# Routing a batch in small pieces: its ranks in an ordinary PSUM bank, its gate and tables spread over the pairs behind it

## The chip, the cores and the metric

The kernel runs on one core of a Trainium2 chip. The metric is the time of one execution on the device in microseconds (us), the median of several runs. The engines have their own instruction queues and run side by side: TensorE (PE; its weight loads are shown as PEld), VectorE (DVE), ScalarE (ACT), GpSimd (POOL) and SyncE (SP), which issues most of the DMA transfers here. Matrix products land in PSUM, in banks of 512 fp32 numbers a partition; everything else lies in SBUF.

## The reference

Three layers, one behind the other, all in fp32:

```
# 1. attention with a memory, B=4 batches, H=8 heads, S=576, D=64
scores = q @ k.T / 8, causal;  a = softmax(scores);  local = a @ v
q_p = where(q > 0, q, exp(q) - 1) + 1
mem = (q_p @ M_prev) / (q_p @ z_prev + 1e-6)
x = g * mem + (1 - g) * local            # g = sigmoid(beta), a head each
# 2. mixture of experts on x as (2304, 512): the best of 8 experts
logits = x @ w_gate;  e = argmax(logits);  gate = softmax(logits)[e]
eom = sigmoid(x @ w_output_gate)
x = gate * eom[e] * (relu(x @ w1[e]) @ w2[e])
# 3. a dense layer
h = relu(x @ w_in);  out = (h * h) @ w_out
```

## The kernel before

**Attention in pairs of heads.** The work of the first layer is cut into 16 pairs: 4 batches, each with 4 pairs of heads. A pair passes four lanes, each a part of the generator `pair`: `prep` (load `kraw` and `qraw`, split them into a high and a low part, `ex` and `rq` on ScalarE), `front` (scores into the banks `sc`, their maxima `negm` on VectorE, the exponentials `a` on ScalarE), `back` (transposes `ptl`, `pt`; the memory product `pm` and its `xm`; the product with v into `pva` and `pvb`, copied to `pvs`; the transposes `ppt` of `pvs`; `tl` on VectorE (line 359), and `xb` = `tl` + `xm` on GpSimd (line 361)), and `end` (store `xb` to `x_dram`, transposes `pxt` to `xTg`, and the gate's product `plg` into `lgT`). In each period of about 12.5 us four successive pairs are worked on at once, one in each lane; the table `PLAN` of 19 steps says in which order the lanes take their steps. A scheduler then sets the final static order on each engine by a model of its own.

**Banks.** Two adjoining banks of PSUM form one wide place (`c.wide`, one buffer): a pair's last-row scores `psl` use it, and the ranks `prank` of a batch use it too. The other six banks are ordinary ones in rotation (`c.bank`).

**Routing of a batch.** When the last pair of a batch has gone through `end`, the next pair's `end` turns the batch's gate products (`plt`), and runs `route_batch` to its end: the one-hot choice `oh`, matrix products that count the ranks of tokens among those of the same expert (`prank`), the gate's softmax (`dd`, `zs`, `eo`, `so`) and its split into three bf16 numbers `sp`, and from the ranks `rk`, `rs` the tables `rblk`, `roff`, `ohoff`. The `yield`s in `route_batch` mean nothing here, since `drain` runs it through at once. The scheduler nevertheless mixes its instructions with those of the pairs.

**Early routing.** After the third batch, `route_early` (begun in the first pair of the fourth batch, finished in its second) chooses the blocks of tokens that the experts start on. It works on the tables of the first three batches: `eeq`, then the five parts of `eval` (two from token numbers `tokv`, three from the split gate `sp`; line 604), then on TensorE two runs of `eperm` with `ohoff` (line 609: the first of the token numbers, the second of the gate), of which `etp`, `egidx` and `esel` are read out, and an indirect DMA on GpSimd's queue gathers the rows `xg` by `egidx`. The transposes `ptx` of `xg` begin the experts, while the last pairs end. The fourth batch's routing and the rest follow among the experts, and then the dense layer.

Of the kernel before, what the change touches and what calls it, by code (L numbers as in the profile page):

```python
# [9 lines left out]
F32 = mybir.dt.float32  # L10
F32R = mybir.dt.float32r
BF16 = mybir.dt.bfloat16
I32 = mybir.dt.int32
# [121 lines left out]
def attention(tc, c, q, k, v, x_dram, pools):  # L135
# [31 lines left out]
    def pair(b, hp, lgT):  # L167
# [56 lines left out]
        def scores(js):  # L224
            banks = [bank(f"sc{js[0]}{h}") for h in range(2)]
            off = [sum((i + 1) * P for i in js[:t]) for t in range(len(js))]
            o, n = off[-1] + js[-1] * P, len(js)
            mask = c.maskd.unsqueeze(1).to_broadcast((P, n, P))
            for h in range(2):
                r = slice(64 * h, 64 * h + 64)  # L230

                def product(qx, kx, start, stop):
                    for i, j in enumerate(js):
                        nk = (j + 1) * P
                        lhs, rhs = (qx[:, h], kx[:, h]) if len(qx.shape) == 3 else (qx[r], kx[r])
                        nc.tensor.matmul(banks[h][:, off[i]:off[i] + nk], lhsT=lhs[:, j * P:nk], rhs=rhs[:, 0:nk],
                                         start=start and i == 0, stop=stop and i == n - 1)

                if stacked:
                    product(q2, k2, True, False)  # L240
                else:
                    product(qh, kh, True, False)
                    product(qh, kl, False, False)
                for i_, j in enumerate(js):
                    nk = (j + 1) * P
                    last = nc.tensor.matmul(banks[h][:, off[i_]:off[i_] + nk], lhsT=qlz[i][:, h, j * P:nk], rhs=kh[:, 0:nk], start=False, stop=False)
                if not stacked:
                    nc.tensor.matmul(banks[h][:, o - (n - 1) * P:o + P], lhsT=c.identb, rhs=mask, start=False, stop=True)
            with tc.issue_after(last.ins):
                for h in range(2) if stacked else ():  # L250
                    nc.tensor.matmul(banks[h][:, o - (n - 1) * P:o + P], lhsT=c.identb, rhs=mask, start=False, stop=True)  # L251
            views = [(banks[h][:, off[i]:off[i] + (j + 1) * P], h, j) for i, j in enumerate(js) for h in range(2)]
            for psv, h, j in views:
                nc.vector.tensor_reduce(out=negm[:, h, j:j + 1], in_=psv, axis=AX.X, op=ALU.max, negate=True)  # L254
            for psv, h, j in views:
                nk = (j + 1) * P
                nc.scalar.activation(a[:, h, aoff[j]:aoff[j] + nk], psv, AF.Exp, bias=negm[:, h, j:j + 1],  # L257
                                     accum_out=ssum[:, h, j:j + 1])
# [93 lines left out]
        for j0, j1 in ((0, 4), (4, 5)):  # L352
            n = j1 - j0
            pt = bank(f"ppt{j0}")
            for j in range(j0, j1):
                transpose(nc, pt[:, (j - j0) * P:(j - j0 + 1) * P], pvs[i][:, j * P:(j + 1) * P], c.ident)
            ptv = pt[:, 0:n * P].rearrange("p (j h e) -> p j h e", j=n, h=2)
            tl = ow.tile([P, 4, 2, D], F32, tag="tl", name="tl")
            nc.vector.tensor_mul(tl[:, 0:n], ptv, clv[:, j0:j1].unsqueeze(3).to_broadcast((P, n, 2, D)))
            xv = xb[:, j0:j1].rearrange("p j (h e) -> p j h e", h=2)  # L360
            (nc.vector if EV["xb"] == "v" or end else nc.gpsimd).tensor_add(xv, tl[:, 0:n], xm[:, j0:j1])
        yield "back"

        if pend:
            b0, l0 = pend.pop()
            logits(b0, l0)
            drain(c.route(b0))
        cs = slice(hp * P, (hp + 1) * P)
        nc.sync.dma_start(out=x_dram[b * S:b * S + 512, cs].rearrange("(j p) f -> p j f", p=P), in_=xb[:, 0:4])
        nc.sync.dma_start(out=x_dram[b * S + 512:(b + 1) * S, cs], in_=xb[0:LAST, 4])  # L370
# [16 lines left out]
        if end:  # L387
            logits(b, lgT)
        elif hp == H // 2 - 1:
            pend.append((b, lgT))  # L390
        elif b == B - 1:
            if hp == RE0:
                next(c.route_early, None)
            elif hp == RE0 + 1:
                for t in c.route_early:
                    if t is None:
                        yield

    pend = []

    def logits(b, lgT):
        pl = bank("plt")
# [12 lines left out]
    def drain(g):  # L415
        for _ in g:
            pass
# [13 lines left out]
    ends = ("end", "back", "front", "prep")  # L431
    for t in range(-2, n):
        lanes = [steps(gens[t + i - 1], ends[i]) if 0 <= t + i - 1 < n else None for i in range(4)]
        for lane in c.plan:
            if lanes[lane] is not None:
                next(lanes[lane], None)
        for lane in lanes[::-1]:
            if lane is not None:
                drain(lane)
# [54 lines left out]
def route_batch(tc, c, b, wk):  # L494
    nc = tc.nc
    cs = slice(b * NB, (b + 1) * NB)
    sh = (P, NB, E)
    lg, lo = c.lg[:, cs, 0:E], c.lg[:, cs, E:2 * E]
    oh = c.oh[:, cs]

    def t3(name):
        return wk.tile([P, NB, E], F32, tag=name, name=name, bufs=1)

    def t2(name, dt=F32):
        return wk.tile([P, NB], dt, tag=name, name=name, bufs=1)

    mx, m2, zs, so = t2("mx"), t2("m2"), t2("zs"), t2("so")
    dd, eo = t3("dd"), t3("eo")
    tt = c.tt[b % 2]
    tx = tt[:, :, 0:E]  # L510
    nc.scalar.activation(eo, lo, AF.Exp, scale=-1.0)
    nc.vector.tensor_reduce(out=mx, in_=lg, axis=AX.X, op=ALU.max)
    mxb = mx.unsqueeze(2).to_broadcast(sh)
    yield "f"
    nc.vector.tensor_tensor(out=tx, in0=lg, in1=mxb, op=ALU.is_equal)
    nc.vector.tensor_sub(dd, lg, mxb)
    yield "f"
    nc.vector.tensor_mul(tx, tx, c.edv)
    yield "f"
    nc.scalar.activation(dd, dd, AF.Exp)  # L520
    nc.vector.tensor_reduce(out=m2, in_=tt, axis=AX.X, op=ALU.max)
    yield "f"
    nc.vector.tensor_tensor(out=oh, in0=tx, in1=m2.unsqueeze(2).to_broadcast(sh), op=ALU.is_equal)
    yield "q"
    pr = c.wide("prank")
    pv = pr[:, 0:NB * E]
    ohf = oh.rearrange("p j e -> p (j e)")
    nc.tensor.matmul(pv, lhsT=c.ones, rhs=c.cum[:, b:b + 1].to_broadcast((P, NB, E)), start=True, stop=False)
    nc.tensor.matmul(pv, lhsT=c.tri, rhs=ohf, start=False, stop=False)
    for j in range(1, NB):  # L530
        nc.tensor.matmul(pr[:, j * E:NB * E], lhsT=c.ones, rhs=ohf[:, 0:(NB - j) * E], start=False, stop=j == NB - 1)
    if b == B - 1:
        pt = c.tot = pr[:, 512:512 + E]
        nc.tensor.matmul(pt, lhsT=c.ones, rhs=c.cum[:, B - 1], start=True, stop=False)
        for j in range(NE_COL, NCOL):
            nc.tensor.matmul(pt, lhsT=c.ones, rhs=c.oh[:, j], start=False, stop=j == NCOL - 1)
    yield "f"
    nc.vector.tensor_reduce(out=zs, in_=dd, axis=AX.X, op=ALU.add)
    nc.vector.tensor_scalar_add(eo, eo, 1.0)
    yield "f"  # L540
    nc.vector.tensor_scalar_add(zs, zs, 1e-9)
    nc.vector.reciprocal(eo, eo)
    yield "f"
    nc.vector.reciprocal(zs, zs)
    nc.vector.tensor_mul(eo, eo, oh)
    yield "f"
    nc.vector.tensor_reduce(out=so, in_=eo, axis=AX.X, op=ALU.add)
    yield "f"
    nc.vector.tensor_mul(zs, zs, so)
    for i in range(3):  # L550
        yield "f"
        nc.vector.tensor_copy(c.sp[:, i, cs], zs)
        if i < 2:
            yield "f"
            nc.vector.tensor_sub(zs, zs, c.sp[:, i, cs])
    yield "f"
    rk = t3("rk")
    rs = t2("rs", I32)
    nc.vector.tensor_mul(rk, pv.rearrange("p (j e) -> p j e", j=NB), oh)
    yield "f"  # L560
    with nc.allow_low_precision("whole numbers"):
        nc.vector.tensor_reduce(out=rs, in_=rk, axis=AX.X, op=ALU.add)
    yield "f"
    nc.vector.tensor_single_scalar(c.rblk[:, cs], rs, 7, op=ALU.logical_shift_right)
    nc.vector.tensor_single_scalar(c.roff[:, cs], rs, P - 1, op=ALU.bitwise_and)
    yield "f"
    nc.vector.tensor_tensor(out=c.ohoff[:, cs], in0=c.ioff.unsqueeze(1).to_broadcast((P, NB, P)),
                            in1=c.roff[:, cs].unsqueeze(2).to_broadcast((P, NB, P)), op=ALU.is_equal)
    if b < B - 1:
        sm = wk.tile([P, E], F32, tag="sm", name="sm", bufs=1)  # L570
        nc.vector.tensor_reduce(out=sm, in_=oh.rearrange("p j e -> p e j"), axis=AX.X, op=ALU.add)
        nc.vector.tensor_add(c.cum[:, b + 1], c.cum[:, b], sm)


def before(tc, wk, tag, c, x):
# [796 lines left out]
```

## Time and profile before

| | |
|---|---|
| median of 3 runs | 914.38 us (913.72 to 916.51) |
| profiled execution | 917.85 us |
| its span, first to last instruction | 916.1 us |
| mean granted clock of TensorE | 0.992 of full speed |
| TensorE busy | 98% of the span |
| attention and early routing | up to about 226 us |
| experts, then the dense layer | from there to the end |

The profile is one execution of the program. A time at the start of a row is counted from the span's start. The trace names the source line of each instruction, the tile it writes and the tiles it reads, and, where an engine sat idle before it, what it waited for.

### The profile page before, as it was taken

The numbers are of one execution on the slowest core, as the hardware profiler recorded it, in microseconds if no ns is written. First come the engines' busy times: TensorE is split into PE (matmuls) and PEld (weight loads), VectorE is DVE, ScalarE is ACT, GpSimd is POOL, SyncE is SP. The second block draws the span as 40 slices with busy tenths as digits, with TensorE's granted clock in tenths as the row PEclk, the third lists the DMA queues.
The fourth block names the chain that finished last, engine by engine and source line by source line (L and its number), as shares of the span: only waits on it lengthen the run. The fifth ranks groups of instructions, "written<-read, shape, count | busy, mean of one in ns | idle before, by whom it ended". The sixth has DMA issues, their size and how long they took to land. (4 is left out here: it accounts for less than half of the span.)

```text
span 916.1 us, 14447 instructions
## 1 busy us (share of the span) xinstructions
PE 893.7 (98%) x5208; PEld 727.8 (79%) x5208; DVE 558.1 (61%) x1083; ACT 469.7 (51%) x934; POOL 196.8 (21%) x268
## 2 busy tenths in 40 slices
PE   7899999999999999999999999999999999999998
PEld 4687778776556889889898788888888888888897
DVE  7777989887586987786777699432223222222232
ACT  5888888864435766465556478432223222222232
POOL 6334333423002043054422004130002000100000
PEclk8999999999999999999999999999999999999999
DMA  9877778655637978756671665120002000100010
GB/s 215 214 187 189 196 196 208 161 128 168 204 124 262 355 276 306 285 200 211 244 242 70 212 234 198 35 92 12 12 12 70 1 1 1 46 1 1 1 46 24
DMA packets 81947, 129.23 MB, mean 141 GB/s; under 512 B 9360, under 2 KB 33936, under 8 KB 81872
## 3 DMA queue, kind: packets, MB, share of 16 engines
q1 hardware_dynamic: 76128, 109.12, 38.9%
q0 software_dynamic: 5744, 19.15, 6.3%
q8 instruction: 43, 0.70, 0.3%
q14 instruction: 32, 0.26, 0.1%
HBM read 109.10 MB, written 15.99 MB: 137 GB/s over the span
## 5 line engine op out<-in xcount | busy, mean ns | idle before, releaser
L1209 DVE SCALAR_TENSOR_TENSOR r<-phf,r 128x512 f32<-128x512 f32 (+1 forms) x64 | 40.0, 625 | 176.9 <-ACT r L1207 176.9
L1207 ACT ACTIVATE r<-phf 128x512 f32<-128x512 f32 (+1 forms) x79 | 43.7, 554 | 185.7 <-PE phf L82 181.4
L863 DVE TENSOR_TENSOR wc<-raw,wc 128x1024 fp32r<-128x1024 f32 x91 | 118.2, 1342 | 14.4 <-ACT wc L861 12.9
L80 PE MATMUL phf<-yT,w 128*128 128x512 f32 (+1 forms) x320 | 119.9, 375 | 0.1
L82 PE MATMUL phf<-yT,w 128*128 128x512 f32 (+1 forms) x320 | 118.1, 369 | 1.4 <-DVE w L1117 1.4
L81 PE MATMUL phf<-yT,w 128*128 128x512 f32 (+1 forms) x320 | 117.8, 368 | 0.0
L861 ACT CAST wc<-raw 128x1024 fp32r<-128x1024 f32 x108 | 106.5, 1058 | 20.1 <-DMA raw<-in_w_dram 8.0
L80 PE MATMUL po<-w,gT 128*128 128x512 f32 x256 | 99.7, 391 | 0.4 <-PEq L1079 0.4
L81 PE MATMUL po<-w,gT 128*128 128x512 f32 x256 | 99.7, 390 | 0.0
L82 PE MATMUL po<-w,gT 128*128 128x512 f32 x256 | 92.7, 390 | 0.0
L257 ACT ACTIVATE a<-sc,negm 128x512 f32<-128x512 f32 (+3 forms) x128 | 66.7, 529 | 15.4 <-DVE negm L254 15.4
L80 PE MATMUL py<-wc,hT 128*128 128x512 f32 x176 | 69.9, 397 | 0.4 <-ACT hT L900 0.4
L82 PEld LDWEIGHTS phf<-yT,w 128*128 128x128 f32 x320 | 60.2, 188 | 12.2 <-DVE w L1117 1.8
L81 PE MATMUL py<-wc,hT 128*128 128x512 f32 x176 | 68.8, 391 | 0.8 <-DVE wc L863 0.8
L80 PEld LDWEIGHTS phf<-yT,w 128*128 128x128 f32 x320 | 60.1, 188 | 11.9 <-ACT w L1115 0.5
L82 PE MATMUL py<-wc,hT 128*128 128x512 f32 x176 | 68.9, 391 | 0.3 <-DVE hT L901 0.3
L81 PEld LDWEIGHTS phf<-yT,w 128*128 128x128 f32 x320 | 60.3, 188 | 10.1
L1214 DVE TENSOR_TENSOR gT<-r,gT 128x512 fp32r<-128x512 f32 x63 | 43.5, 690 | 40.2 <-ACT gT L1213 39.9
L254 DVE TENSOR_REDUCE negm<-sc 128x1 f32<-128x512 f32 (+3 forms) x128 | 55.1, 483 | 19.9 <-PE sc L251 19.8
L863 POOL TENSOR_TENSOR wc<-raw,wc 128x1024 fp32r<-128x1024 f32 x17 | 43.9, 2587 | 90.5 <-ACT wc L861 82.8
L80 PEld LDWEIGHTS po<-w,gT 128*128 128x128 f32 x256 | 48.1, 188 | 11.0 <-issue 0.8
L82 PEld LDWEIGHTS po<-w,gT 128*128 128x128 f32 x256 | 48.0, 188 | 10.3
(356 smaller groups left out, 1961.8 us busy)
## 6 DMA issues: line engine op xcount, KB each, us to landing
raw<-in_w_dram SPq DMA_DIRECT2D x64, 1024.0 KB, 5.5
q<-qh SPq DMA_DIRECT2D x60, 128.0 KB, 2.5
kraw<-in_k_dram SPq DMA_DIRECT2D x16, 288.0 KB, 4.6
qraw<-in_q_dram SPq DMA_DIRECT2D x16, 288.0 KB
vts<-in_v_dram SPq DMA_DIRECT2D x16, 256.0 KB, 3.6
qlz<-ql SPq DMA_DIRECT2D x32, 128.0 KB, 2.8
x_dram<-xb SPq DMA_DIRECT2D x16, 256.0 KB, 5.0
k<-kh SPq DMA_DIRECT2D x30, 128.0 KB, 3.4
```

The lines of the kernel that those rows point to most:

```text
L80: nc.tensor.matmul(out, lhsT=lh, rhs=rh, start=start, stop=False)
L81: nc.tensor.matmul(out, lhsT=lh, rhs=rl, start=False, stop=False)
L82: return nc.tensor.matmul(out, lhsT=ll, rhs=rh, start=False, stop=stop)
L254: nc.vector.tensor_reduce(out=negm[:, h, j:j + 1], in_=psv, axis=AX.X, op=ALU.max, negate=True)
L257: nc.scalar.activation(a[:, h, aoff[j]:aoff[j] + nk], psv, AF.Exp, bias=negm[:, h, j:j + 1], accum_out=ssum[:, h, j:j + 1])
L861: nc.scalar.copy(wc[:, 0, ks], raw[:, ks])
L863: eng.tensor_sub(wc[:, 1, ks], raw[:, ks], wc[:, 0, ks].bitcast(F32))
L1207: nc.scalar.activation(r[:, 0:nt], ph[:, 0:nt], AF.Relu)
L1209: nc.vector.scalar_tensor_tensor(out=r[:, 0:nt], in0=ph[:, 0:nt], scalar=0.0, in1=r[:, 0:nt], op0=ALU.max, op1=ALU.mult)
L1214: nc.vector.tensor_sub(gT[:, 1, 0:nt], r[:, 0:nt], gT[:, 0, 0:nt].bitcast(F32))
```

## The change

Three batches (all but the last) get their routing differently:

- `prank` is an ordinary bank, not the wide one, and the ranks `rk` and `rs` are read as soon as the products are done; the running count `cum` is made at the same place. Then `route_batch` pauses (`yield "c"`).
- What is left (softmax, split, tables) stays in the list `slow`. Behind every third step of `PLAN` one small piece of it is issued, and `tc.issue_after` keeps it behind the latest maximum `negm` or product `tl` on VectorE (`c.anchor`).
- What the third batch has left by the second pair of the fourth batch is issued there at once, ahead of the rest of `route_early`.

The fourth batch is routed as before, in the wide bank. The numbers computed are the same.

```diff
@@ scores
-                nc.vector.tensor_reduce(out=negm[:, h, j:j + 1], in_=psv, axis=AX.X, op=ALU.max, negate=True)
+                c.anchor = nc.vector.tensor_reduce(out=negm[:, h, j:j + 1], in_=psv, axis=AX.X, op=ALU.max, negate=True)
@@ pair, lane back
-            nc.vector.tensor_mul(tl[:, 0:n], ptv, clv[:, j0:j1].unsqueeze(3).to_broadcast((P, n, 2, D)))
+            c.anchor = nc.vector.tensor_mul(tl[:, 0:n], ptv, clv[:, j0:j1].unsqueeze(3).to_broadcast((P, n, 2, D)))
@@ pair, lane end
             logits(b0, l0)
-            drain(c.route(b0))
+            slow.append(c.route(b0))
+            for t in slow[-1]:
+                if t == "c":
+                    break
...
             elif hp == RE0 + 1:
+                drain(slow.pop())
                 for t in c.route_early:
@@ the lanes
-        for lane in c.plan:
+        for at_, lane in enumerate(c.plan):
             if lanes[lane] is not None:
                 next(lanes[lane], None)
+            if slow and at_ % 3 == 0:
+                with tc.issue_after(c.anchor.ins):
+                    next(slow[-1], None)
@@ route_batch
-    pr = c.wide("prank")
+    pr = c.wide("prank") if b == B - 1 else c.bank("prank")
...
+    def ranks():
+        nc.vector.tensor_mul(rk, pv.rearrange("p (j e) -> p j e", j=NB), oh)
+        yield "f"
+        with nc.allow_low_precision("whole numbers"):
+            nc.vector.tensor_reduce(out=rs, in_=rk, axis=AX.X, op=ALU.add)
+        yield "f"
+
+    yield "f"
+    if b < B - 1:
+        sm = wk.tile([P, E], F32, tag="sm", name="sm", bufs=1)
+        nc.vector.tensor_reduce(out=sm, in_=oh.rearrange("p j e -> p e j"), axis=AX.X, op=ALU.add)
+        nc.vector.tensor_add(c.cum[:, b + 1], c.cum[:, b], sm)
+        yield from ranks()
+        yield "c"
     nc.vector.tensor_reduce(out=zs, in_=dd, axis=AX.X, op=ALU.add)
```

In the pieces below the lines of the changed kernel are 3 to 14 higher for the same code (359 and 254 are the same, 604 is 618, 385 is 388, 639 is 653).

TensorE, ahead of the third batch's products `prank`, as the difference of the two orders; `psl` are the last-row scores of the last pair, and `pt` are transposes of `a`.

```order
 L76 MATMUL ptl<-ident,al 128x128 x4
-L76 MATMUL pt_3123<-ident,a 128x128 x4
+L76 MATMUL pt_3123<-ident,a 128x128 x2
+L80 MATMUL psl<-kh,qlasth_122 128x288
+L76 MATMUL pt_3123<-ident,a 128x128 x2
 L76 MATMUL pt_3129<-ident,a 128x128 x3
```

Before, the same `psl` stood behind `prank`, that is one period later, behind the next `plg`, `ppt` and `ptl`. In the first two batches one `psl` each moves in the same way.

SP, the DMA issues around a store of `xb` two periods behind the store with which the first batch ends; `kraw` and `qraw` are the loads of keys and queries, `vts` those of v. Before:

```order
L369 DMA x_dram<-xb 128x4x128
L370 DMA x_dram<-xb 64x128
L176 DMA kraw<-in_k_dram 128x576
L176 DMA qraw<-in_q_dram 128x576
L217 DMA vts_126<-in_v_dram 64x128
L216 DMA vts_126<-in_v_dram 128x4x128
```

After, one period later:

```order
L372 DMA x_dram<-xb 128x4x128
L373 DMA x_dram<-xb 64x128
L176 DMA qraw<-in_q_dram 128x576
L176 DMA kraw<-in_k_dram 128x576
L217 DMA vts_127<-in_v_dram 64x128
L216 DMA vts_127<-in_v_dram 128x4x128
```

The load of the queries, which followed that of the keys of the same pair, now follows the pair of stores one period later.

VectorE behind the third batch's first `tl`, in the first pair of the fourth batch; `zs`, `eo` and `so` are the gate's softmax, `eni` and `efull` belong to `route_early`. Before:

```order
L359 TENSOR_TENSOR tl<-ppt_3304,cl 128x512
L359 TENSOR_TENSOR tl<-ppt_3312,cl 128x128
L673 CAST eni<-etot 128x8
L165 COPY aTs_128<-ptl 128x2x2x64
L266 TENSOR_REDUCE negm<-psl 128x1
L319 SCALAR_TENSOR_TENSOR cl<-ssum,gneg 128x10
L676 TENSOR_SCALAR efull<-eni 128x8
```

After:

```order
L359 TENSOR_TENSOR tl<-ppt_3292,cl 128x512
L359 TENSOR_TENSOR tl<-ppt_3300,cl 128x128
L567 RECIPROCAL zs<-zs 128x5
L568 TENSOR_TENSOR eo<-eo,oh 128x40
L687 CAST eni<-etot 128x8
L165 COPY aTs_128<-ptl 128x2x2x64
L319 SCALAR_TENSOR_TENSOR cl<-ssum,gneg 128x10
L570 TENSOR_REDUCE so<-eo 128x5
L690 TENSOR_SCALAR efull<-eni 128x8
```

Two operations of the softmax came in behind `tl` and the maximum of `psl` is gone from there; `so` and six more operations up to the last `sp` follow further down, among the maxima of the same period.

VectorE one period later, where `route_early` ends; `eval` with `tokv` or `sp` are its five parts, `etp` and `etf` lead to the gather's index `egidx`, `cl` is the scale of the pair then in lane back. Before:

```order
L604 TENSOR_TENSOR eval<-eeq,tokv 128x90 x2
L604 TENSOR_TENSOR eval<-eeq,sp 128x90
L385 TENSOR_TENSOR lgT<-lgT,plg 128x160
L604 TENSOR_TENSOR eval<-eeq,sp 128x90 x2
L254 TENSOR_REDUCE negm<-sc_3487 128x1
L254 TENSOR_REDUCE negm<-sc_3488 128x1
L359 TENSOR_TENSOR tl<-ppt_3500,cl 128x512
L359 TENSOR_TENSOR tl<-ppt_3508,cl 128x128
L625 COPY etp<-eperm_3533 128x12
L639 COPY esel<-eperm_3549 128x5
L319 SCALAR_TENSOR_TENSOR cl<-ssum,gneg 128x10
```

After:

```order
L618 TENSOR_TENSOR eval<-eeq,sp 128x90 x2
L388 TENSOR_TENSOR lgT<-lgT,plg 128x160
L254 TENSOR_REDUCE negm<-sc_3483 128x1
L254 TENSOR_REDUCE negm<-sc_3484 128x1
L359 TENSOR_TENSOR tl<-ppt_3496,cl 128x512
L359 TENSOR_TENSOR tl<-ppt_3504,cl 128x128
L575 CAST sp<-zs 128x5
L639 COPY etp<-eperm_3533 128x12
L319 SCALAR_TENSOR_TENSOR cl<-ssum,gneg 128x10
L618 TENSOR_TENSOR eval<-eeq,sp 128x90
L643 SCALAR_TENSOR_TENSOR etf<-etp 128x5
```

The last part of `sp` and the last of the five `eval` now stand behind `tl`, the `eval` behind `cl` too. On TensorE the second run of `eperm` still stands ahead of `ptl`, as before.

## Rows read from the trace of the kernel before

**Rows 1.** The page's first part: busy us, share of the span, instructions.

```profile
PE 893.7 (98%) x5208; PEld 727.8 (79%) x5208; DVE 558.1 (61%) x1083; ACT 469.7 (51%) x934; POOL 196.8 (21%) x268
```

**Rows 2.** TensorE's waits from 47 to 215: us in all, times, longest.

```profile
PE ppt L76 <- ACT pvs L165: 2.2, 4, 1.1
```

**Rows 3.** Timeline, TensorE: start, us, engine, line, operation; in brackets idle before.

```profile
87.17 0.66 PE L76 MATMUL ppt<-ident,pvs 128*128 128x128 f32 x4 [1.13 <-ACT pvs L165]
...
99.88 0.66 PE L76 MATMUL ppt<-ident,pvs 128*128 128x128 f32 x4 [0.30 <-ACT pvs L165]
...
100.94 0.38 PE L80 MATMUL psl<-kh,qlasth 128*128 128x288 f32 x1
...
101.87 0.74 PE L76 MATMUL pt<-ident,a 128*128 128x128 f32 x5
...
151.47 0.65 PE L76 MATMUL ppt<-ident,pvs 128*128 128x128 f32 x4 [0.39 <-ACT pvs L165]
```

**Rows 4.** Timeline, ScalarE: an exponential of the queries that waits for their load.

```profile
85.45 0.68 ACT L192 ACTIVATE ex<-qraw 128x576 f32<-128x576 f32 x1 [1.87 <-DMA qraw<-in_q_dram]
```

**Rows 5.** Timeline, SP's queue: a load of queries directly behind its keys.

```profile
110.52 0.35 SPq L176 DMA_DIRECT2D qraw<-in_q_dram  x1
```

**Rows 6.** Windows: length, busy PE, PEld, DVE, ACT, POOL (instructions), clock, DMA, GB/s.

```profile
202.10:214.70 12.60, 12.60 (x109) 10.26 (x108) 12.21 (x52) 8.32 (x27) 1.90 (x3) 1.00 0.17 46
```

**Rows 7.** Timeline, VectorE, in the first and the third batch's routing.

```profile
102.74 0.49 DVE L564 TENSOR_SCALAR rblk<-rs 128x5 int32<-128x5 int32 x1
...
199.81 0.20 DVE L545 TENSOR_TENSOR eo<-eo,oh 128x40 f32<-128x40 f32 x1
199.92 0.19 DVE L544 RECIPROCAL zs<-zs 128x5 f32<-128x5 f32 x1
...
204.97 0.75 DVE L266 TENSOR_REDUCE negm<-psl 128x1 f32<-128x576 f32 x1
205.64 0.22 DVE L319 SCALAR_TENSOR_TENSOR cl<-ssum,gneg 128x10 f32<-128x10 f32 x1
...
214.30 0.41 DVE L604 TENSOR_TENSOR eval<-eeq,sp 128x90 bf16<-128x90 bf16 x2
214.74 1.02 DVE L254 TENSOR_REDUCE negm<-sc 128x1 f32<-128x384 f32 x2
...
216.66 1.13 DVE L319 SCALAR_TENSOR_TENSOR cl<-ssum,gneg 128x10 f32<-128x10 f32 x1
...
218.32 0.10 DVE L632 TENSOR_SCALAR egidx<-etf 128x5 uint32<-128x5 f32 x1
```

**Rows 8.** Timeline, GpSimd: the additions `xb`, a big and a small one each.

```profile
101.92 1.71 POOL L361 TENSOR_TENSOR xb<-tl,xm 128x512 f32<-128x512 f32 x2
...
204.53 1.72 POOL L361 TENSOR_TENSOR xb<-tl,xm 128x512 f32<-128x512 f32 x2 [10.97 <-DVE tl L359]
...
216.49 1.69 POOL L361 TENSOR_TENSOR xb<-tl,xm 128x512 f32<-128x512 f32 x2 [9.53 <-DVE tl L359]
```

**Rows 9.** Groups by form, GpSimd: busy us, mean ns of one, idle before, releaser.

```profile
L361 POOL TENSOR_TENSOR xb<-tl,xm 128x512 f32<-128x512 f32 x2 | 2.6, 1284 | 20.5 <-DVE tl L359 20.5
```

**Rows 10.** Timeline, TensorE, early in the kernel and around the end of `route_early`.

```profile
34.34 0.67 PE L76 MATMUL ppt<-ident,pvs 128*128 128x128 f32 x4 [1.91 <-ACT pvs L165]
...
215.14 0.90 PE L609 MATMUL eperm<-eval,ohoff 128*128 128x12 bf16 x30
...
218.63 0.84 PE L76 MATMUL pt<-ident,a 128*128 128x128 f32 x6 [0.39 <-DVE esel L642]
...
225.83 0.66 PE L76 MATMUL ptx<-ident,xg 128*128 128x128 f32 x4 [1.32 <-DMA xg<-x_dram,egidx]
```

**Rows 11.** Windows (columns as in rows 6): TensorE's granted clock is third from last.

```profile
35.00:36.00 1.00, 1.00 (x8) 1.00 (x6) 1.00 (x3) 1.00 (x3) 0.88 (x3) 0.50 1.10 294
...
38.00:38.50 0.50, 0.50 (x4) 0.50 (x4) 0.41 (x2) 0.26 (x1) 0.50 (x2) 0.73 0.91 184
...
225.00:226.00 1.00, 0.17 (x2) 0.18 (x3) 0.00 (x0) 0.00 (x0) 0.00 (x0) 1.00 0.49 193
```

More of the change, by code (lines that the diff above doesn't have):

```diff
@@ L397, in pair @@
                         yield
-    pend = []
+    pend, slow = [], []
     def logits(b, lgT):
@@ L536, in route_batch @@
             nc.tensor.matmul(pt, lhsT=c.ones, rhs=c.oh[:, j], start=False, stop=j == NCOL - 1)
-    yield "f"
+    rk = t3("rk")
+    rs = t2("rs", I32)
+    def ranks():
[4 more added lines that the diff above has]
+        yield "f"
+    yield "f"
+    if b < B - 1:
[4 more added lines that the diff above has]
+        yield "c"
     nc.vector.tensor_reduce(out=zs, in_=dd, axis=AX.X, op=ALU.add)
@@ L556, in route_batch @@
     yield "f"
[L557 to L563, printed above, removed]
+    if b == B - 1:
+        yield from ranks()
     nc.vector.tensor_single_scalar(c.rblk[:, cs], rs, 7, op=ALU.logical_shift_right)
@@ L568, in route_batch @@
                             in1=c.roff[:, cs].unsqueeze(2).to_broadcast((P, NB, P)), op=ALU.is_equal)
[L569 to L572, printed above, removed]
 def before(tc, wk, tag, c, x):
```

## The prediction

> **What bounds the kernel now.** I read the page's busy times first: TensorE is busy 98% of the span, VectorE 61%, ScalarE 51%, GpSimd 21% [rows 1]. So only what TensorE waits for, or what lowers its clock, can move the time. The second view is therefore TensorE's waits from 47 to 215 us, where the batches' routing lies between the pairs: one line, 2.2 us in four waits, the longest 1.1 [rows 2]. **2.2 us, 0.24% of the time, is all that the stage from 47 to 215 us can give back.**
>
> The third view, TensorE's timeline, shows that these waits stand at `ppt`, the transposes of `pvs` [rows 3]. They follow the copy of `pvs` on ScalarE, which is queued behind `ex`, and `ex` waits about 2 us for `qraw` [rows 4]: a late load of the queries, not the wide bank. On SP's queue a query load is late where it stands behind the stores of `x_dram`. Before, this happens in five periods after 70 us, and four of them show a wait: 2.2/5 = 0.43 us for each on average. An early load, as the one at 110.52 [rows 5], follows the load of the keys and brings no wait.
>
> **The edits in batches one and two.** The ranks leave the wide bank, so `psl` no longer waits for them. Before, one `psl` slides by up to 24 us to 100.94 [rows 3], and nothing waits for it; it costs TensorE the same 0.93 us wherever it stands (from 100.94 to the next row's 101.87). The move itself is worth nothing. It has two side effects. TensorE comes 0.9 us later to the `ppt` of the period in which `psl` was missing, so the waits at 99.88 (0.30) and 151.47 (0.39) [rows 3] are covered: −0.7. And two query loads, the one at 110.52 and its like in the next batch, move a period on and behind the stores (second order piece): two more late loads at 0.43, +0.9 (from 0 if they are covered to 2 × 1.13 by the longest wait). Sum: **+0.2**. The tables in pieces cost no more here, since VectorE is busy 61% [rows 1] and nothing on TensorE waits for it in this stage [rows 2].
>
> **The third batch.** Here VectorE has no cover. From 202.10 to 214.70 it is busy 12.21 of 12.60 us, while GpSimd is busy 1.90 [rows 6]; `route_early` runs there and needs the third batch's tables at its end.
> First, `psl` moves from behind `plg` to ahead of it (as in the first order piece). VectorE's stretch begins with the maxima of scores at 202.10, which TensorE now gives 0.9 us later, at 203.0. TensorE has that 0.9 back by 206, when the old `psl` is missing; VectorE can't use it, since it is full.
> Second, what VectorE has to do there: nine small operations of the softmax move in, which before stood ahead of 202. They start about 0.1 us apart (199.81 and 199.92 [rows 7]): +0.9. The maximum of `psl` (0.75 at 204.97) and one `eval` (0.2 of the pair at 214.30) move out [rows 7]: −0.95.
> Third, a block. `cl` at 216.66, 10 numbers a partition, takes 1.13 us, and the same `cl` at 205.64 takes 0.22 [rows 7]. The first lies beside GpSimd's `xb` additions, which start at 216.49 [rows 8]; the big one lasts 1.284 [rows 9] and so ends at 217.77, where `cl` ends (217.79). The second `cl` comes behind the 0.75 of the `psl` maximum, when the big addition from 204.53 [rows 8] is about over. After the change that maximum is gone, and `eo`×`oh`, with both inputs in SBUF, stands directly behind `tl` (third order piece). GpSimd's addition starts with the second `tl`; `eo`×`oh` comes some 0.2 later and is held to its end: +1.1. If it isn't held, `cl` behind it may be. The stretch then needs 12.21 + 0.9 − 0.95 + 1.1 = 13.26 us from 203.0, so the maxima of `sc_3483` come at 216.3 and not at 214.74: **+1.55**.
>
> `rblk` at 102.74, 5 numbers a partition and one input in SBUF, takes 0.49 to 103.23 [rows 7]; GpSimd's big addition from 101.92 ends at 101.92 + 1.28 = 103.20 [rows 8]. The Trainium skill (SBUF — State Buffer, "Who interferes with whom") says that two inputs in SBUF contend with a GpSimd instruction that reads SBUF, that copies, casts and scalar operations can too in some modes, and that the pair of ports is held for the whole instruction; it fits both rows. By that rule the `sp` cast ahead of `etp` would be held as well, with `cl` behind it, some 0.2 us more than the sum below, and without such a rule the block's terms would be zero.
>
> **The tail of route_early.** Now the last part of `sp`, and with it the last `eval`, come behind `tl`, where before all `eval` were done ahead of the maxima (fourth order piece). TensorE's second run of `eperm` needs that `eval`. With +1.55, `cl` starts at 216.66 + 1.55 + 0.1 for the cast = 218.3, held to 219.35; the next operation with two SBUF inputs is the last `eval`, held by the second, small addition. That one ends 0.4 behind the first (216.49 + 1.69 = 218.18 against 217.77 before), so at 219.73; `eval` takes 0.2: 219.9. TensorE began its second run in the middle of the 0.90 us from 215.14 [rows 10], at 215.6. It would now be **idle for 4.3 us**, with `ptl`, `pt` and all behind them queued behind it. Of that, the wait of 0.39 at 218.63 is covered. The next meeting point is `ptx` at 225.83, which waits 1.32 for the gathered `xg` [rows 10]; TensorE was there at 224.5 and is now there at 224.5 + 4.3 − 0.4 = 228.4. The gather's index `egidx` comes 0.3 behind `eval`, at 220.2 and not 218.32 [rows 7], so `xg` comes at 225.83 + 1.9 = 227.7, ahead of TensorE. `ptx`: 228.4 − 225.83 = **+2.6**. Without any block the stretch ends at 203.0 + 12.16 = 215.2, the last `eval` at about 217.5, and `ptx` starts at 226.0: +0.2. With `cl` and `eval` held alone it is +1.5. I take 2.6, since `cl` shows the block in this very place.
>
> **The clock.** After the wait of 1.91 us at 34.34 [rows 10] the granted clock is 0.50, that is 1.2 of 2.4 GHz, from 35 to 36, and the half microsecond from 38.0 has a mean of 0.73, so it rises in the middle of that [rows 11]: about 3.4 us at half speed, a loss of 1.7. After the 1.32 us of idle at 225.83 it stays at 1.00 [rows 11]. An idle of 4.3 is beyond the first, so I add **+1.7**.
>
> From `ptx` on, the order is unchanged, and the experts and the dense layers are bound by TensorE, so the shift stays. Sum: 0.2 + 2.6 + 1.7 = **+4.5**. The profiled execution took 917.85 us, 3.5 above the median of 914.38; the same edits on the median give 914.4 + 4.5 = **918.9**.
>
> **Rivals.**
> - *The clock holds.* The fall at 35 us came early in the kernel, in a stage with other waits around it; the long idle at 219 may be judged otherwise. Then +2.8: 917.2, chance 0.20.
> - *No block in the third batch.* VectorE's ops could miss GpSimd's additions by a few tenths, since 0.9 us of shifts lie in between. For it: the `cl` at 205.64 was free. Against it: `tl` starts both the addition and the operations behind it, so they move together. Then +0.2 + 0.2 = +0.4: 914.8; with `cl` held alone and the clock full it is 0.2 + 1.5: 916.1. Chance 0.18.
> - *Faster.* The two newly late loads cost nothing, because `psl` ahead of `ppt` covers them as it covers the old ones, and all four waits of [rows 2] go: −2.2. This decides once the tail costs under 2.2, so it needs the tail unblocked, +0.2 of it: −2.0, 912.4. Against it: `psl` moves in one period of four only, and the wait of 1.13 at 87.17 lies in a period that keeps its loads. Chance 0.12.
>
> The forecast has 0.50. A change within 0.3% (2.7 us, up to 917.1 and down to 911.6) is about what a measurement of this kernel can't tell from none. Slower by more: the forecast and half of the first rival (its 917.2 lies on the line), less 0.06 for a block or a clock loss smaller than taken, 0.54. Faster by more: half of the third rival, where a term outside the views adds the 0.7 that it lacks, 0.06. Within: the rest, 0.40. The range's low end is the second rival with the two late loads free, 914.8 − 0.9 = 913.9; its top is the forecast with both late loads at 1.13, 918.9 + 1.4 = 920.3. Left out is most of the third rival and little above.
>
> **What would show it.** After the change: no `ppt` wait in the periods of `plt`; TensorE idle some 2 to 4.3 us at `eperm` near 216, released by `eval` on VectorE; `eo`×`oh` near 205.6 at about 1.2 us; `cl` near 218 at about 1.1; the granted clock 0.50 in a stretch behind 220. The prediction is wrong if `eperm` runs without a wait, or if the stages from 230 on differ by over 1 us.

## The result and the profile after

The changed kernel takes 920.47 us (median of 7 runs, 917.83 to 921.89) against 915.16 us (7 runs). The medians differ by 5.3 us; the ratio of the mean times is 1.0053, 95% interval 1.0042 to 1.0064, or 4.9 us more (3.8 to 5.9), and the sums below go by that. The prediction said 918.9 for a median of 914.4, 4.5 us more, and slower. The profiled execution took 920.54 us, its span 918.8.

The page's busy times after the change, which answer to [rows 1]: TensorE has the same work, in a longer span.

```profile
PE 894.0 (97%) x5208; PEld 727.4 (79%) x5208; DVE 564.5 (61%) x1083; ACT 469.8 (51%) x934; POOL 196.0 (21%) x268
```

Where the time went is read from the starts of the 16 `plg` groups on TensorE's timeline, one for each pair, and of the first `ptx`. A batch's routing lies in the stretches 4 to 6, 8 to 10 and 12 to 14; 6 to 8 and 10 to 12 are the two periods behind the first and second. The numbers are us, each rounded difference against the profile of before in brackets.

| stretch, by `plg` number | before | after |
|---|---|---|
| start to 2nd | 59.5 | 58.4 (−1.0) |
| 2nd to 4th | 25.0 | 24.9 (0) |
| 4th to 6th, first batch | 27.3 | 27.2 (−0.1) |
| 6th to 8th | 25.0 | 25.8 (+0.8) |
| 8th to 10th, second batch | 26.6 | 26.7 (+0.1) |
| 10th to 12th | 25.0 | 25.8 (+0.8) |
| 12th to 14th, third batch | 25.0 | 27.1 (+2.1) |
| 14th to first `ptx`, tail | 12.6 | 15.0 (+2.4) |
| first to fifth `ptx` | 51.5 | 49.9 (−1.6) |
| from there to the end | 638.8 | 638.0 (−0.8) |

The single profiles differ by only 2.7 us of span, since that of before had a slower start and a clock fall near 268 us that this one lacks (its row stands with the clock, below). The stretches from the 2nd `plg` to `ptx` add up to +6.1, of which (1 − 0.57) × 4 = 1.7 is a clock fall in the tail (the windows are shown below).

TensorE's waits from 47 to 230 us (in all, times, longest), which answer to [rows 2]:

```profile
PE eperm L623 <- DVE eval L618: 2.7, 1, 2.7
PE ppt L76 <- ACT pvs L165: 2.2, 3, 1.0
PE sc L236 <- ACT a L257: 1.2, 2, 0.6
PE pm L328 <- DVE lg L411: 0.9, 3, 0.3
PE pt L76 <- ACT a L257: 0.4, 2, 0.2
```

The wait at `eperm` is the one that was forecast. Those at `sc`, `pm` and `pt` are new and were not. The line of `ppt` is again 2.2, though the waits at 99.88 and 151.47 are gone: a new one of 0.83 stands at 47.52, ahead of the stretches that count here. TensorE's timeline shows where they stand; the last row answers to `ptx` in [rows 10], which no longer waits:

```profile
93.66 1.35 PE L328 MATMUL pm<-mbd,qpad 128*128 128x130 f32 x10 [0.29 <-DVE lg L411]
...
118.17 0.44 PE L236 MATMUL sc<-k,q 128*128 128x256 f32 x2 [0.61 <-ACT a L257]
...
204.87 0.63 PE L76 MATMUL ptl<-ident,al 128*128 128x128 f32 x4
205.75 1.11 PE L76 MATMUL pt<-ident,a 128*128 128x128 f32 x7 [0.25 <-ACT a L257]
206.85 0.50 PE L236 MATMUL sc<-k,q 128*128 128x512 f32 x1
...
221.11 0.54 PE L623 MATMUL eperm<-eval,ohoff 128*128 128x18 bf16 x15 [2.68 <-DVE eval L618]
...
230.95 0.66 PE L76 MATMUL ptx<-ident,xg 128*128 128x128 f32 x4
```

VectorE's timeline after the change, in the period behind the first batch and in the third batch and the tail (these answer to [rows 7]):

```profile
113.78 0.45 DVE L575 CAST sp<-zs 128x5 bf16<-128x5 f32 x1
114.15 0.16 DVE L582 TENSOR_SCALAR rblk<-rs 128x5 int32<-128x5 int32 x1
114.22 1.26 DVE L583 TENSOR_SCALAR roff<-rs 128x5 int32<-128x5 int32 x1
...
207.00 1.27 DVE L568 TENSOR_TENSOR eo<-eo,oh 128x40 f32<-128x40 f32 x1
...
217.50 1.02 DVE L254 TENSOR_REDUCE negm<-sc 128x1 f32<-128x384 f32 x2
...
219.23 1.25 DVE L575 CAST sp<-zs 128x5 bf16<-128x5 f32 x1
...
220.48 0.42 DVE L319 SCALAR_TENSOR_TENSOR cl<-ssum,gneg 128x10 f32<-128x10 f32 x1
220.82 0.24 DVE L618 TENSOR_TENSOR eval<-eeq,sp 128x90 bf16<-128x90 bf16 x1
```

and GpSimd's work beside them (its additions answer to [rows 8]; `kl` is the low part of a pair's keys):

```profile
112.78 1.42 POOL L185 TENSOR_TENSOR kl<-kraw,kh 128x576 fp32r<-128x576 f32 x1 [1.47 <-issue]
114.16 1.71 POOL L361 TENSOR_TENSOR xb<-tl,xm 128x512 f32<-128x512 f32 x2
...
206.93 1.70 POOL L361 TENSOR_TENSOR xb<-tl,xm 128x512 f32<-128x512 f32 x2 [8.37 <-DVE tl L359]
...
219.20 1.67 POOL L361 TENSOR_TENSOR xb<-tl,xm 128x512 f32<-128x512 f32 x2 [10.57 <-DVE tl L359]
```

`roff`, `eo` and the second `sp`, of 5 or 40 numbers a partition, each start within 0.1 us of a big addition's start and end with it (206.93 + 1.28 = 208.21; `eo` ends at 208.27). The first `sp` ends with `kl`, at 114.2. Operations that last to the end of GpSimd's in this way are called held, and the stretch a hold. The pieces were tied to `tl`, and `tl` is what starts the addition, so they meet by construction.

### The profile page after: what moved, and what is told of

It reads as the page before. It is cut to its first block, busy times and chain, and to the rows that moved or that the text cites. A ratio compares the mean times of both kernels' runs of the same rounds, so it can differ in the third digit from the quotient of the medians.

```text
span 918.8 us, 14442 instructions
## 1 busy us (share of the span) xinstructions
PE 894.0 (97%) x5208; PEld 727.4 (79%) x5208; DVE 564.5 (61%) x1083; ACT 469.8 (51%) x934; POOL 196.0 (21%) x268
## 5 line engine op out<-in xcount | busy, mean ns | idle before, releaser
L877 DVE TENSOR_TENSOR wc<-raw,wc 128x1024 fp32r<-128x1024 f32 x91 | 118.3, 1344 | 14.4 <-ACT wc L875 12.6
```

The lines of the kernel that those rows point to most:

```text
L877: eng.tensor_sub(wc[:, 1, ks], raw[:, ks], wc[:, 0, ks].bitcast(F32))
```

## The experiments

Each ratio is to the kernel before, run on the same chip, with its 95% interval. The table gives the stretches of each profile against before, in us as above. A profile is one execution, and all are set against one profile of before. The `ppt` wait of 1.13 at 87.17 goes from 0.41 to 1.17 in the profiles where its load of queries has not moved, and the wait of `ptx` for `xg`, 1.32 before, is 1.00 to 1.16 on one chip and 0.50 to 0.57 on two others. So single differences of some 0.8 in the columns 4–6 and tail can be chance.

| | 4–6 | 6–8 | 8–10 | 10–12 | 12–14 | tail | ratio |
|---|---|---|---|---|---|---|---|
| changed kernel | −0.1 | +0.8 | +0.1 | +0.8 | +2.1 | +2.4 | 1.0053 |
| bank only | +1.4 | 0 | +2.0 | 0 | +1.8 | −0.2 | 1.0056 |
| pieces, wide bank | +0.1 | +0.8 | +0.2 | +0.8 | +1.1 | +1.7 | 1.0058 |
| third batch at once | −0.1 | +0.9 | 0 | +0.8 | +1.8 | −0.3 | 1.0031 |
| a piece at every step | +1.4 | −0.1 | +1.8 | 0 | +2.0 | −0.4 | 1.0066 |
| pieces behind maxima | +0.7 | +1.4 | +0.8 | +1.5 | +2.3 | +0.3 | 1.0081 |
| two batches | −0.6 | +0.8 | +0.2 | +0.8 | 0 | −0.8 | 1.0008 |
| `xb` on VectorE | −0.4 | +0.8 | +0.2 | +0.8 | +1.7 | +0.7 | 1.0064 |
| three `qraw` buffers | −0.4 | 0 | +0.3 | 0 | 0 | −0.8 | 0.9997 |
| calm places | −0.6 | 0 | −0.4 | 0 | 0 | −0.8 | 0.9983 |
| calm, three buffers | −1.2 | +0.1 | −0.4 | 0 | 0 | −0.8 | 0.9984 |

**The ordinary bank alone**, on the kernel before:

```diff
-    pr = c.wide("prank")
+    pr = c.wide("prank") if b == B - 1 else c.bank("prank")
```

> The kernel before with the ordinary bank for the ranks of three batches, and nothing else: the routing still runs through at once, every part of sp and eval stands ahead of tl as before, and the query loads stay where they were. First theory (the prediction's: the loss is the tail of route_early): no wait at eperm, the ppt waits of 0.30 and 0.39 gone, within 0.7 us of the kernel before, 914.5 to 915.5. Rival (the ordinary bank itself costs: the rank product holds one of six banks for about a period, so pm waits for the copies lg and sc for the exponentials a): three waits of about 0.3 to 0.45 at pm and two of about 0.6 at sc as in the changed kernel, 2 us slower, about 917.

Measured: 921.11, ratio 1.0056 (1.0043 to 1.0069), 5.1 us slower. The first theory falls: with no `eperm` wait at all, the bank alone costs as much as the whole change. The rival's waits are there (three of 0.29 at `pm`, two of 0.81 and two of 0.28 at `sc`), but the cost is over twice the 2 us that it gave, and the third batch costs 1.8 with only small waits in it. TensorE and VectorE in this run:

```profile
106.72 0.44 PE L236 MATMUL sc<-k,q 128*128 128x256 f32 x2 [0.81 <-ACT a L257]
...
206.93 0.63 PE L76 MATMUL ptl<-ident,al 128*128 128x128 f32 x4
207.81 1.11 PE L76 MATMUL pt<-ident,a 128*128 128x128 f32 x7 [0.25 <-ACT a L257]
208.91 0.50 PE L236 MATMUL sc<-k,q 128*128 128x512 f32 x1
```

```profile
100.82 1.17 DVE L564 TENSOR_SCALAR rblk<-rs 128x5 int32<-128x5 int32 x1
...
102.77 1.25 DVE L555 TENSOR_TENSOR zs<-zs,sp 128x5 f32<-128x5 f32 x1
...
209.37 0.93 DVE L319 SCALAR_TENSOR_TENSOR cl<-ssum,gneg 128x10 f32<-128x10 f32 x1
```

In the first two batches the loss comes with holds again. The ranks are read earlier than before, so `rblk`, between the maxima and `tl`, meets GpSimd's `kl` (100.55 to 101.96) and takes 1.17, where before it took 0.49; a step of the split, `zs`, starts with the big addition (102.73) and takes 1.25. The second batch has the same pair (1.16 at 154.34, 1.26 at 156.29). The waits at `sc` for `tl` (0.28) and for `a` (0.81) follow them.

From `ptl` to the next `sc` it is 1.98 us here and in the changed kernel. The timeline of before has 2.02 for the same stretch, with `psl` in it:

```profile
202.54 0.63 PE L76 MATMUL ptl<-ident,al 128*128 128x128 f32 x4
202.92 0.38 PE L80 MATMUL psl<-kh,qlasth 128*128 128x288 f32 x1
...
203.84 0.96 PE L76 MATMUL pt<-ident,a 128*128 128x128 f32 x7
204.56 0.48 PE L236 MATMUL sc<-k,q 128*128 128x512 f32 x1
```

So `psl` in its late place cost nothing: it filled 0.9 us in which `pt` has to wait for the exponentials (0.25 of that shows as idle). And the maximum of `psl` kept `cl` out of GpSimd's way (0.22 in [rows 7], 0.93 here).

**The pieces with the ranks in the wide bank**: `c.wide` for all batches, the rest as changed.

> The change with its small pieces, but with the ranks left in the wide bank. First theory: sp and the last eval stand behind tl in the third batch as in the changed kernel, so eperm waits 2 to 2.7 us and the granted clock falls to 0.50 for some 3 us behind it: 3 to 4.5 us slower than before, 918 to 919.7, most of the change's loss. Rival (the bank costs): no waits at pm and sc, so at least 2 us of the loss are gone, 917 or less.

Measured: 920.57, ratio 1.0058 (1.0044 to 1.0073): the first theory, a little above its range; the rival's 917 falls. The pieces too cost all of it alone: 0.8 in each of the periods behind the first two batches, 1.1 in the third, 1.7 in the tail. The 1.7 is again a clock fall (means of 0.54 and 0.61 from 220 to 224). There are no waits at `pm`, so those belong to the bank; the two at `sc` are there, so those belong to the pieces.

```profile
118.71 0.45 PE L236 MATMUL sc<-k,q 128*128 128x256 f32 x2 [0.61 <-ACT a L257]
...
220.35 0.57 PE L623 MATMUL eperm<-eval,ohoff 128*128 128x18 bf16 x15 [2.33 <-DVE eval L618]
```

```profile
219.02 1.11 DVE L319 SCALAR_TENSOR_TENSOR cl<-ssum,gneg 128x10 f32<-128x10 f32 x1
```

The last row is VectorE's. Here the cast of `sp` ran ahead of the addition (0.16 at 218.82), and `cl` was held in its stead, as the prediction had it.

In the third batch and the tail, without the clock, bank and pieces add up: 1.6 for the bank alone, 1.2 for the pieces alone, 2.8 for both. In the stretches 4 to 12 they do not: 3.3, 1.9 and 1.7. With the pieces spread, `rblk` and `zs` no longer stand beside `kl` and `xb` in the batch's own period, as they do with the bank alone.

**The third batch at once**, its ranks in the ordinary bank:

```diff
             for t in slow[-1]:
-                if t == "c":
+                if t == "c" and b0 < B - 2:
                     break
```

> The change, but the third batch's remaining pieces run through at once as before (its ranks stay in the ordinary bank). First theory: no wait at eperm, the clock holds behind 216, and only the +0.2 of the first two batches is left: 915 to 916. Rival (the bank costs): the waits at pm (3) and sc (2) remain, about 2 us slower than before: 917.

Measured: 918.74, ratio 1.0031 (1.0020 to 1.0042), 2.8 us slower: nearer to the rival's 2 than to the first theory. The tail's loss is gone, and the third batch still costs 1.8.

**A piece at every step** (`if slow:` in place of every third step):

> The change with a small piece issued behind every step of the plan instead of every third, so that all three parts of sp and all eval stand ahead of the second tl in the third batch, and eo times oh stands ahead of the first. First theory: the eperm wait goes or falls under 1 us and the clock holds: 915 to 916.5. Rival (the bank costs): 917 to 918 with the waits at pm and sc still there.

Measured: 921.32, ratio 1.0066 (1.0052 to 1.0080), above both ranges. The `eperm` wait is gone as said, but the stretches are those of the bank alone: crowded into one period, the routing costs 1.4 to 2.0 a batch, and it meets GpSimd in the same way (`sp` 1.24 at 100.43 by `kl`, `rblk` 1.27 at 102.38 by `xb`). The spread over the periods does help the bank (−0.1 against +1.4 in the first batch), and gives 0.8 back behind it.

**Pieces behind the maxima only**: `tl` no longer sets `c.anchor`.

> The change with the small pieces kept behind the maxima negm alone, no longer behind the products tl. Theory (a piece behind tl starts together with GpSimd's xb addition and is held by it): in the first two batches no piece takes over 0.5 us behind tl (in the changed kernel roff took 1.26 there), and the two waits of 0.61 at sc near 118 and 171 go: 1 to 1.5 us faster than the changed kernel, about 919.5. The last eval still stands behind tl, so it is held for about 1 us and eperm still waits some 2 us. Rival (the pieces cost by their number, or sc waits because six banks are short): the waits at sc stay at 0.6, 920.5 or more.

Measured: 921.68, ratio 1.0081 (1.0067 to 1.0095), the slowest of all; my expectation was wrong. GpSimd's `kl` = `kraw` − `kh` reads SBUF too, and runs ahead of `tl`. The pieces now met that one, and then held `tl` itself back. VectorE, then GpSimd:

```profile
100.81 1.17 DVE L568 TENSOR_TENSOR eo<-eo,oh 128x40 f32<-128x40 f32 x1
101.90 0.88 DVE L359 TENSOR_TENSOR tl<-ppt,cl 128x512 f32<-128x512 f32 x2
...
113.83 1.23 DVE L575 CAST sp<-zs 128x5 bf16<-128x5 f32 x1
```

```profile
100.51 1.42 POOL L185 TENSOR_TENSOR kl<-kraw,kh 128x576 fp32r<-128x576 f32 x1 [2.35 <-issue]
...
113.63 1.41 POOL L185 TENSOR_TENSOR kl<-kraw,kh 128x576 fp32r<-128x576 f32 x1 [1.47 <-issue]
```

**Two batches only**, the third wholly as before (wide bank, at once, ranks last):

> The change in the first two batches, the third batch wholly as before the change (wide bank, all at once, ranks read last). Theory (in the third batch the ordinary bank moves psl away from where it covered TensorE's wait for the exponentials, which cost 1.8 to 2 us with or without pieces): the third batch and the tail are as before, and only the first two batches' 0.8 each is left: 1.4 us slower than before, 916.5 to 917. Rival (the third batch's bank costs nothing and the loss lies in the first two batches): as with the third batch at once in an ordinary bank, 918.5.

Measured: 915.70, ratio 1.0008 (0.9997 to 1.0019). The third batch is back to 25.0, as expected, and the 1.4 that was expected lies within the interval. The rival's 918.5 falls. The 0.6 and the 0.8 less in the columns 4–6 and tail are the two waits that vary from profile to profile (0.41 at `ppt`, 0.54 for `xg`).

**The `xb` additions of two pairs on VectorE**:

```diff
-            (nc.vector if EV["xb"] == "v" or end else nc.gpsimd).tensor_add(xv, tl[:, 0:n], xm[:, j0:j1])
+            (nc.vector if EV["xb"] == "v" or end or b == B - 1 and hp < 2 else nc.gpsimd).tensor_add(xv, tl[:, 0:n], xm[:, j0:j1])
```

> The changed kernel with the xb additions of the first two pairs of the fourth batch on VectorE instead of GpSimd, so that nothing of GpSimd's reads SBUF behind these two tl. Theory (GpSimd's addition holds VectorE's operations): eo times oh takes 0.2 and not 1.27, the sp cast behind the next tl 0.16 and not 1.25, cl 0.2; VectorE gets 0.7 and 0.3 more of additions for each pair, so the time is within 1 us of the changed kernel and eperm waits 2 to 3 us. Rival (these operations are slow by themselves or wait for something else): they stay over 1 us and eperm waits 4 us or more.

Measured: 919.65, ratio 1.0064 (1.0048 to 1.0079). `eo`×`oh` fell from 1.27 to 0.16 with GpSimd's addition away: the hold is shown. The `tl` of the tail turned out to be the next pair's, whose `xb` is still on GpSimd; there `sp` slipped in ahead of the addition and the hold went to the next in line, `cl`. VectorE, then GpSimd:

```profile
208.35 0.16 DVE L568 TENSOR_TENSOR eo<-eo,oh 128x40 f32<-128x40 f32 x1
...
220.48 0.16 DVE L575 CAST sp<-zs 128x5 bf16<-128x5 f32 x1
220.63 1.16 DVE L319 SCALAR_TENSOR_TENSOR cl<-ssum,gneg 128x10 f32<-128x10 f32 x1
```

```profile
220.50 1.76 POOL L361 TENSOR_TENSOR xb<-tl,xm 128x512 f32<-128x512 f32 x2 [20.59 <-DVE tl L359]
```

**Three `qraw` buffers in the kernel before** (`load("q", q, fr, 3)`):

> The kernel before with three buffers for qraw instead of two, so that every load of queries stands ahead of the stores of xb on SP's queue; nothing of the change. Theory (the ppt waits come from late query loads): the four ppt waits between 47 and 215 us, 2.2 us in all, go: 1.5 to 2.2 us faster than before, 913.5 to 914. Rival (the wait moves to another place, since the copy of pvs waits for other work on ScalarE): 915 to 916.

Measured: 914.68, ratio 0.9997 (0.9987 to 1.0007): no change that can be measured, the rival. All `ppt` waits are gone, so late loads did cause them; but TensorE now waits elsewhere in the same two batches, 2.0 us in all (the second pair of waits, 0.44 and 0.55, stands at 156 and 160):

```profile
104.14 0.37 PE L80 MATMUL psl<-kh,qlasth 128*128 128x288 f32 x1 [0.44 <-ACT al L267]
108.47 2.70 PE L341 MATMUL pva<-aTs,vts 128*64 128x448 f32 x20 [0.55 <-DVE xTg L165]
```

**Pieces in calm places.** Two batches as above, but pieces are issued only behind the maxima of the score blocks 3 and (1,0), four at a time, so that none stands beside `kl` or `xb`:

```diff
-                c.anchor = nc.vector.tensor_reduce(out=negm[:, h, j:j + 1], in_=psv, axis=AX.X, op=ALU.max, negate=True)
+                red = nc.vector.tensor_reduce(out=negm[:, h, j:j + 1], in_=psv, axis=AX.X, op=ALU.max, negate=True)
+            if js != (2,):
+                c.anchor, c.calm = red, True
...
-            if slow and at_ % 3 == 0:
+            if slow and c.calm:
                 with tc.issue_after(c.anchor.ins):
-                    next(slow[-1], None)
+                    for _ in range(4):
+                        next(slow[-1], None)
+            c.calm = False
```

> The change in the first two batches alone (third batch as before), with the small pieces issued only behind the maxima of the score blocks 3 and (1,0), four at a time, so that on VectorE none stands between the maxima of block 2 and the end of GpSimd's kl and xb operations. Theory (pieces lose time where GpSimd reads SBUF, beside kl or xb): no piece takes over 0.5 us, the waits of 0.61 at sc near 118 and 171 go, and the 0.8 us in the period behind each of the two batches with them: 1 to 1.5 us faster than the same without this placing (915.7), 914 to 915. Rival (pieces delay VectorE by their number wherever they stand): the 0.8 us in each of the two periods stays.

Measured: 913.19, ratio 0.9983 (0.9973 to 0.9992): faster than both kernels, by 1.6 us against before (0.7 to 2.5 by the interval). The same pieces, elsewhere in the same period, take 0.16 each, and the 0.8 behind each batch is gone, the waits at `sc` too. VectorE:

```profile
116.08 0.17 DVE L586 TENSOR_SCALAR rblk<-rs 128x5 int32<-128x5 int32 x1
116.16 0.16 DVE L587 TENSOR_SCALAR roff<-rs 128x5 int32<-128x5 int32 x1
...
117.49 0.16 DVE L579 CAST sp<-zs 128x5 bf16<-128x5 f32 x1
```

The ranks of these two batches are in the ordinary bank here, and the stretches 4 to 12 are no longer than before. So in these batches the bank as such costs no more than its 0.29 at `pm`. Two things moved along with the pieces: `ohoff`, 0.8 us of real work, left the place ahead of the maxima too, and the two query loads that had become late (at 120 and 172) are early again. The loads come behind the waits at `sc` and can't be their cause; how much of the 0.8 was hold and how much the place of `ohoff` was not tried alone. Nor is it shown where the 1.6 come from: the waits from 47 to 215 explain 0.5 (the `ppt` waits at 99.88, 138.68 and 151.47 gone, two of 0.29 at `pm` new), and the tail's 0.8 stands in the profile with three buffers as well, whose time is that of before.

**Calm places and three `qraw` buffers together**:

> The run above with three buffers for qraw as well, so that no load of queries stands behind the stores. Theory: no piece is held, and no ppt wait is left; psl in its early place no longer waits for al and leaves VectorE free for xTg, so the waits that took the place of the ppt waits with three buffers alone (0.44 at psl, 0.55 at pva, in two batches) go too: 2 to 2.5 us faster than the kernel before, about 913. Rival (new waits take their place): 914.5 to 915.5.

Measured: 914.20, ratio 0.9984 (0.9971 to 0.9997). No `ppt`, `psl` or `pva` wait is left from 47 to 215 us, only two of 0.29 at `pm`. The time lies between the theory and the rival. By the ratio it equals the run without the third buffer: the further 0.6 that the profile gains in the first batch doesn't show in the times.

## Why the prediction held, and where it didn't

**The total** was right (4.5 said, 4.9 measured), and the third batch and its tail carried most of it, as said. That it came so close is in part luck: one term was too small by 1.5, another came out right with over half of it from the bank, whose 0.9 TensorE was to have back, and the third, the clock, can't be told to within its own size.

**Batches one and two, +0.2: wrong.** The stretches from the 4th to the 12th `plg` cost +1.7 in all. The `ppt` waits at 99.88 and 151.47 did go; the two newly late query loads cost nothing, since no `ppt` wait follows them. The step that failed is "The tables in pieces cost no more here, since VectorE is busy 61%". The pieces stand behind `tl`, where GpSimd holds them: `sp` 0.45 by `kl` and `roff` 1.26 by `xb` at 114, so the maxima of the next scores come late, and `sc` waits 0.61 in each of the two periods. In the calm places the 0.8 is gone with the holds (and with `ohoff` out of the way). The prediction had found the hold in the trace and applied it in the third batch only. The bank adds 0.29 at `pm` in each batch, which no batch has whose ranks stay in the wide bank.

**The third batch.** The hold of `eo`×`oh` was 1.27 (1.2 said). The maxima of the scores ahead of the tail came 2.1 later, by the distance from the 12th `plg` (28.6 against 26.5), where 1.55 was said. "TensorE has that 0.9 back by 206" failed, and with it "it costs TensorE the same 0.93 us wherever it stands": TensorE lost it at once, at `pt`, waiting for exponentials, a wait that `psl` used to fill (2.02 us from `ptl` to `sc` with it, 1.98 without). So not only VectorE was short; the bank alone, without a piece more on VectorE, costs 1.8 here.

**The tail.** The wait at `eperm` was forecast at 4.3 and measured at 2.68. The last `eval` came as said behind `sp` and `cl`, but the big addition held the cast (1.25) and not `cl`, and `cl` (0.42) ended with the small one, at 220.9. The Trainium skill (SBUF — State Buffer, "Who interferes with whom") says that casts can contend with GpSimd in some modes; the trace agrees, with 1.25 here against 0.16 where GpSimd is quiet. TensorE had lost its time already, in the third batch, and was at `eperm` 2 us later than the sum took it to be. Third batch and tail without the clock come to 2.1 + 2.4 − 1.7 = 2.8 against the 2.6 of the prediction. That agreement is in good part luck: by the runs above the pieces alone make 1.2 of it, and the bank, whose 0.9 TensorE was to have back, 1.6.

**The clock, +1.7: right in the profile, open in the mean.** In the profile it fell as forecast. Windows (length, busy PE, PEld, DVE, ACT, POOL, clock third from last) from 222 to 226 and around a lull of TensorE at 269 to 272, where it waits 0.8 and 1.5 us within 3 us; then before, behind the same lull:

```profile
222.00:226.00 4.00, 4.00 (x24) 3.96 (x23) 1.26 (x4) 2.14 (x5) 3.09 (x4) 0.57 1.06 376
268.99:272.99 4.00, 2.51 (x27) 1.80 (x28) 3.79 (x14) 1.99 (x2) 0.00 (x0) 1.00 0.51 190
```

```profile
267.00:268.00 1.00, 1.00 (x19) 0.88 (x16) 1.00 (x3) 0.00 (x0) 0.00 (x0) 0.50 1.04 406
```

So before has a fall that the changed kernel's profile has not. Over the runs the mean granted clock is 0.9954 (7 runs) against 0.9961 (56 runs of before, with the experiments): 0.0007 × 917 = 0.6 us. The scatter of the 7 runs (0.993 to 0.998) leaves anything from nothing to the full 1.7. The other terms, 1.7 + 2.8 = 4.5, and the 4.9 measured with its interval don't settle it either. In these two profiles the fall in the tail (1.7) and the one that is missing near 268 (1.6) cancel; how they weigh over the runs is not shown.

**The rivals.** A held clock behind the wait was not seen in this profile, but it was in two of the experiments' (2.66 us with `xb` on VectorE, 2.27 with the pieces behind maxima). The rival without a block is refuted by the holds of 1.27 and 1.25. The changed kernel was not faster, though its two late loads did cost nothing, as the third rival said.

**The signs.** Those at `ppt`, `eperm`, `eo`×`oh` and the clock came true; `cl` near 218 at 1.1 did not (0.42 at 220.48, since the cast came first). One sign of being wrong came up as well: the stages behind the first `ptx` differ by 2.4, not under 1. Of that, 1.6 is the clock fall of before near 268; the other 0.8 lies within what the profiles of the experiments show there (0 to 0.9).

**What stays open.** Why `lg` delays `pm` with the ordinary bank was not separated from the rotation of the six banks. How the 1.8 of the third batch in the run with the bank alone splits between the hole that `psl` filled and the held `cl` is argued from rows (0.9 and 0.7), not tried alone. How the 0.8 behind each of the first two batches splits between holds and `ohoff` was not tried alone. Why an idle of one length lowers the clock in one execution and not in another, no run here settles.

## What to carry to other kernels

Ask what else starts on the instruction to which small work is tied: an anchor that releases another engine's operation puts the small work right beside it, and here an operation of 0.16 us took 1.27. An instruction that stands late and looks displaced may be filling a wait; before it is moved back, look at what its neighbours wait for. Read the small operations again after any change of order: with the bank alone no piece was moved, and two holds a batch came in all the same. And where a hold is found at one place of a loop, look for it in every period.

## What the runs showed of the hardware

A VectorE operation of 5 to 40 numbers a partition takes about 0.2 us alone and up to 1.27 beside a 1.28 us addition of GpSimd or a 1.41 us subtraction; a cast, a scalar operation on integers, a product of two tensors and the scale `cl` were all held, to the end of GpSimd's instruction. Of several in the queue the one that comes first pays: the cast in the tail of the changed kernel (1.25), and `cl` where the cast had started 0.02 us ahead of the addition (1.16). That casts with one input were held I had expected least. Not every hold costs time: in the changed kernel's first batch `cl` took 0.96 at 101.96, and no wait on TensorE follows it in that period.

In these profiles the granted clock does not follow from the length of one idle. After 2.68 us at `eperm` it fell, and after 2.33 with the ranks in the wide bank; after 2.66 in the run with `xb` on VectorE it stayed full:

```profile
222.00:226.00 4.00, 3.99 (x48) 4.00 (x49) 2.03 (x8) 2.00 (x5) 2.87 (x4) 1.00 1.10 394
```

The lull of 0.8 and 1.5 us near 268 stands in all twelve profiles, and half speed followed it in six: before, the bank alone, the third batch at once, a piece at every step, and both with calm places. In the changed kernel and in that with the wide bank the clock had fallen at the tail, and it held here. In the other four, pieces behind maxima, two batches, `xb` on VectorE and three `qraw` buffers, it fell at neither place. These four were run on one chip, and each of the other eight has a fall at one of the two places, so a difference of chips is not ruled out.
